# GateLoop attention and a feed-forward block: fp32 weights through the load queue, rotated tiles in one operation, a new order table

## The chip, the cores and the metric

The kernel runs on one core of a Trainium2 chip. The metric is the device time of one execution in microseconds (us), the median of several runs. A core has a matrix engine (PE; its weight loads are shown apart as PEld), a vector engine (DVE), a scalar engine (ACT), a general engine (POOL) and a queue engine (SP) that does nothing here but issue DMA transfers. Sixteen DMA engines carry all transfers.

## What is computed

The inputs q, k, v, a_re, a_im are 4 batches x 8 heads x 768 steps x 48 in fp32. The recurrence keeps a complex 48 x 48 state for each batch and head, decays its rows by the gate a (magnitude capped at 0.999), adds k times v and reads it with q. The heads side by side give x (384 wide), which goes through a normalization, two matrix products with a rectifier between them, and a residual sum:

```
S_re, S_im = ar*S_re - ai*S_im + outer(k_t, v_t), ar*S_im + ai*S_re
y_t = q_t @ S_re                                   # x: the heads' y_t side by side
xn  = (x - mean) / sqrt(var + 1e-6) * g_ln
out = x + max(xn @ w_ch1, 0) @ w_ch2               # 384 -> 1536 -> 384
```

The two weights are fp32 in memory, 2.36 MB each. The kernel computes with them in bf16.

## The kernel before

**Work and names.** A batch of 768 steps is six chunks of 128 steps. Two chunks are a pair `P`, so there are 12 pairs and 24 chunks `n`; `X` is a pair and its part, and only pair 0 has two parts (`PARTS`), split over heads. For each pair the gate gives decays and angles: `ln`, `iv`, `r`, `r2`, `u`, `l`, `lc` work out log magnitude and tangent, `dec` sums the logs on PE, `e` and `en` are its exponentials, `th` and `ph` the angles and their sums, `car` hands the angle to the next pair, `sin`, `abs`, `cos` (or `qt`, `cos` in pairs 0 to 3) fill `trig`.

**Rotated tiles.** `ke` and `qe` are k and q times their decay. `ks` and `qs` (L291 through the helper `tt`) hold, for each head, 48 columns times cosine, 16 zero columns, 48 times sine, 16 zeros. Each is written by two operations of 128x768 elements, `.0` with cosine and `.1` with sine.

**Chunk work.** `kT`, `qT` turn `ks`, `qs` on PE into PSUM (L592) and `ksT`, `qsT` copy them out. Where the table gives `ksT` or `qsT` to SP, the PE step and the copy are left out and a transposing DMA does it (L597). `am` (L615) is the score matrix, `atm` masks it, `gm` (L643) and `G` carry the state, `y` (L665, L668) is the output, `x` its copy, `xtr` and `xT` turn it, `bn` and `rstd` are the normalization, `mm1` (L719), `relu`, `mm2` (L740), `ot`, `st` the rest.

**Loads.** `k`, `q`, `vf` (192 KB each, L403) and `are`, `aim` (384 KB, L444) are issued by SP. They move in rows of 192 and 384 bytes. The weights come in six parts `wl.0` to `wl.5`: three column blocks of `w1b`, three row blocks of `w2b`. POOL issues them as DMAs (L363, L365), and these turn fp32 into bf16 on the way. `wp` and `wc` then fold the mean and `g_ln` into `w1b`, so `wl.0` to `wl.2` must be there before the first `mm1`, and `wl.3` to `wl.5` before `mm2`.

**Order.** Nothing is scheduled at run time. The string `PLAN` lists 1,087 steps with the engine of each (`P`, `A`, `V`, `G`, `S` for PE, ACT, DVE, POOL, SP) and its PSUM bank; each engine runs its own steps in the order of the string and waits at a step until its inputs are there. `@name` holds a POOL step back until the named step of DVE is done. `warm` steps are PE products whose result is not used. `RINGS` gives the number of buffers of each tile; a step that writes a buffer waits for the last user of its previous content. SP is one such engine: a load behind a transposing DMA whose `ks` isn't ready waits with it.

Of the kernel before, what the change touches and what calls it, by code (L numbers as in the profile page):

```python
# [57 lines left out]
en.2.0:A4 ks.0.1.0:G wc.0.1:V3 qT.0:P0 iv.3.0:A wc.0.0:V3 v.0:G kT.0:P1 e.2.0:A4 wc.0.2:V3 warm.71:P2
pad.qs.1:G qsT.0:A0 qT.1:P4 ksT.0:V1 r.3.0:G vf.1.1:S kT.1:P5 qsT.1:V4 car.1.0:A6 am.0:P2 ksT.1:V5 vf.1.0:S
ph.2.0:P0 atm.0:V2 qe.1.0.1:G am.1:P4 q.2.1:S tab.trig.3:A sin.1.0:A6 ke.1.0.0:G atm.1:V4 gm.0:P2 sin.2.0:A0  # L60
are.4.0:S qt.1.0:P6 ke.1.0.1:G y.0:P3 cos.1.0:A6 qt.2.0:P0 G.0:V2 wp.2:P4 ks.1.0.1:V x.0:A3 q.2.0:S cos.2.0:A0
y.1:P5 ks.1.0.0:V xtr.0:P3 qs.1.0.1:V gm.1:P2 aim.4.0:S x.1:A5 kT.3:P6 qs.1.0.0:V th.3.0:A kT.2:P5 G.1:V2
v.1:G@qs.1.0.0 xtr.1:P7 xT.0:A3 qT.2:P0 ksT.2:V5 k.2.0:S xT.1:A7 qT.3:P1 wl.3:G ksT.3:V6 mm1.0.0.1:P2 qsT.3:V1
mm1.0.0.0:P2 r2.3.0:G qsT.2:V0 tab.log.4:A ln.4.0:A am.3:P6 wc.2.1:V4 mm1.0.1.1:P0 relu.0.0:A2 wl.4:G atm.3:V6
mm1.0.1.0:P0 u.3.0:A gm.2:P5 qe.2.0.1:G wc.2.2:V4 am.2:P2 relu.0.1:A0 ph.3.0:P6 wl.5:G wc.2.0:V4 iv.4.0:A
G.2:V5 mm1.0.2.1:P0 qe.2.0.0:G atm.2:V2 y.3:P4 r.4.0:G mm1.0.2.0:P0 car.3.0:V6 y.2:P2 x.3:V4 tab.trig.5:A
sin.3.0:A6 mm2.0.0:P3 x.2:V2 relu.0.2:A0 xtr.3:P4 qs.2.0.0:G bn.1:V qt.3.0:P6 gm.3:P5 mm2.1.0:P2 xT.3:V4
cos.3.0:A6 k.2.1:S xtr.2:P4 mm2.0.1:P3 r2.4.0:A pad.ks.2:G xT.2:V4 q.3.0:S G.3:V5 qs.2.0.1:G mm2.1.1:P2
th.4.0:A bn.3:V mm1.1.0.1:P0 vf.2.0:S bn.2:V mm1.1.2.1:P6 bn.0:V are.6.0:S rstd.1:G mm1.1.2.0:P6 tab.log.6:A
u.4.0:A l.3.0:V mm2.0.2:P3 rstd.0:G k.3.1:S relu.1.2:A6 mm1.1.0.0:P0 l.4.0:V mm1.1.1.1:P4 relu.1.0:A0 q.3.1:S  # L70
lc.3.0:V ke.2.0.1:V mm1.1.1.0:P4 ke.2.0.0:V are.5.0:S dec.3.0:P6 relu.1.1:A4 ks.2.0.1:V mm2.2.0:P0 lc.4.0:V
ks.2.0.0:V ln.6.0:A mm2.2.1:P0 k.3.0:S ot.0:V3 e.3.0:A6 mm2.2.2:P0 vf.2.1:S en.3.0:A6 qT.4:P1 qe.3.0.0:V
kT.4:P3 qe.3.0.1:V iv.6.0:A st.0:S dec.4.0:P4 qs.3.0.1:V aim.5.0:S qsT.4:A1 mm2.1.2:P2 qs.3.0.0:V ksT.4:V3
dps.3:P6 ke.3.0.1:G@qs.3.0.0 en.4.0:A4 qT.5:P7 vf.3.1:S ot.2:V0 mm2.3.0:P1 ln.5.0:A ke.3.0.0:G qsT.5:V7
q.4.0:S qT.6:P0 e.4.0:A4 decc.3:V6 ks.3.0.1:V kT.5:P3 oa.1:A2 am.4:P6 qsT.6:V0 vf.3.0:S v.2:G@ks.3.0.1
ph.4.0:P4 iv.5.0:A ksT.5:V3 ks.3.0.0:G k.4.0:S atm.4:V6 gm.4:P0 car.4.0:A4 am.5:P2 G.4:A0 aim.6.0:S mm2.3.1:P1
atm.5:V2 r.5.0:G kT.6:P0 qT.7:P6 q.4.1:S y.5:P7 tab.trig.7:A sin.4.0:A4 qsT.7:V6 kT.7:P2 ot.1:G k.4.1:S x.5:A7
y.4:P3 ksT.7:V2 th.5.0:A mm2.3.2:P1 v.3:G x.4:V3 vf.4.0:S abs.4.0:A4 dps.4:P6 ksT.6:V0 qe.4.0.0:G xtr.4:P7
am.7:P2 r2.5.0:A xT.4:V7 q.5.0:S xtr.5:P0 decc.4:V6 am.6:P4 r.6.0:G ot.3:V1 xT.5:A0 ph.5.0:P6 cos.4.0:A
vf.4.1:S atm.6:V4 mm1.2.1.1:P0 sin.5.0:A6 are.7.0:S ke.4.0.0:G atm.7:V2 y.6:P4 mm1.2.1.0:P0 abs.5.0:A6  # L80
ke.4.0.1:G gm.6:P5 x.6:A4 are.8.0:S mm1.2.2.0:P2 G.6:V5 cos.5.0:A qe.4.0.1:G xtr.6:P4 relu.2.1:V0 y.7:P6
gm.7:P5 q.5.1:S ks.4.0.1:G x.7:A6 mm1.2.2.1:P2 bn.4:V r2.6.0:A xtr.7:P0 mm1.2.0.1:P6 vf.5.0:S xT.7:V0
relu.2.2:A2 xT.6:V4 mm1.2.0.0:P6 qs.4.0.0:G G.7:V5 st.1:S th.6.0:A bn.7:V mm1.3.0.0:P0 k.5.0:S relu.2.0:V6
mm1.3.1.0:P2 ks.4.0.0:G aim.7.0:S mm1.3.2.1:P4 bn.5:V mm1.3.2.0:P4 tab.log.8:A u.5.0:A bn.6:V rstd.2:G
mm1.3.1.1:P2 u.6.0:A qs.4.0.1:V mm2.5.0:P6 l.5.0:V relu.3.2:A4 qsT.9:S mm2.4.0:P7 mm1.3.0.1:P0 lc.5.0:V
relu.3.1:A2 l.6.0:V ksT.8:S mm2.4.1:P7 ln.7.0:A relu.3.0:V0 dec.5.0:P4 vf.5.1:S mm2.4.2:P7 e.5.0:A4 q.6.1:S
lc.6.0:V v.4:V mm2.5.1:P6 en.5.0:A4 st.3:S qe.5.0.1:V dec.6.0:P2 ot.4:V7 k.5.1:S iv.7.0:A mm2.6.0:P0 en.6.0:A2
r.7.0:G k.6.1:S qT.8:P1 kT.9:P7 ln.8.0:A qsT.8:V1 mm2.5.2:P6 aim.8.0:S e.6.0:A2 ksT.9:V7 am.8:P4 qe.5.0.0:G
r2.7.0:A mm2.7.0:P1 atm.8:V4 st.4:S gm.8:P7 rstd.3:A qs.5.0.0:G st.2:S am.9:P2 u.7.0:A G.8:V7 aim.9.0:S
mm2.6.1:P0 atm.9:V2 ph.6.0:P4 ke.5.0.0:G k.6.0:S qs.5.0.1:V y.9:P2 tab.trig.9:A th.7.0:A gm.9:P7 l.7.0:V  # L90
y.8:P3 q.6.0:S mm2.7.1:P1 abs.6.0:A4 x.9:V2 ke.5.0.1:G@l.7.0 mm2.6.2:P0 are.9.0:S car.6.0:A4 G.9:V7 sin.6.0:A4
mm2.7.2:P1 x.8:V3 qe.6.0.1:V oa.6:A0 qT.11:P7 vf.6.0:S bn.8:V xtr.8:P2 xtr.9:P3 ph.7.0:P4 lc.7.0:V xT.9:A3
q.7.1:S xT.8:V2 cos.6.0:A ks.5.0.0:V mm1.4.1.1:P2 abs.7.0:V4 vf.6.1:S ke.6.0.1:G@ks.5.0.0 car.7.0:A4
mm1.4.1.0:P2 sin.7.0:A4 ks.5.0.1:V dps.6:P0 qsT.10:S oa.7:A1 v.5:V mm1.4.0.1:P4 relu.4.1:A2 ke.6.0.0:V
mm1.4.0.0:P4 qsT.11:V7 ot.6:G@ke.6.0.0 k.7.1:S kT.11:P1 relu.4.0:V4 mm1.4.2.0:P2 ks.6.0.0:G k.7.0:S
mm1.4.2.1:P2 decc.6:V0 tab.log.10:A ln.9.0:A ksT.11:V1 mm2.8.0:P7 q.7.0:S relu.4.2:A2 ot.5:V6 qe.6.0.0:G
kT.10:P0 bn.9:V am.11:P4 k.8.1:S iv.8.0:A qs.6.0.0:G mm2.9.0:P6 ksT.10:V0 rstd.4:A st.6:S dec.7.0:P2 atm.11:V4
iv.9.0:A st.5:S mm2.8.1:P7 k.8.0:S e.7.0:A2 r.8.0:V gm.10:P0 mm2.9.1:P6 en.7.0:A2 ks.6.0.1:V am.10:P4 G.10:A0
qs.6.0.1:V ksT.13:S mm2.8.2:P7 r.9.0:V qT.13:P0 mm2.9.2:P6 atm.10:V4 qsT.12:S ke.7.0.0:G@r.9.0 tab.trig.11:A
th.9.0:A y.11:P1 kT.12:P2 ke.7.0.1:G th.8.0:A x.11:V1 q.8.0:S y.10:P3 qsT.13:V0 ksT.12:A2 xtr.11:P1 ks.7.0.1:G  # L100
ph.8.0:P4 x.10:V3 cos.7.0:A xT.11:V1 xtr.10:P0 ph.9.0:P2 abs.8.0:V4 xT.10:A0 ks.7.0.0:G ot.8:V7 mm1.5.0.1:P0
# [704 lines left out]
```

## Time and profile before

| | |
|---|---|
| time, median of 3 runs | 192.32 us (192.16 to 192.44) |
| span of the profiled execution, first to last instruction | 190.8 us |
| what lies around the span, median less span | 1.5 us |
| busy: PE, DVE, ACT, POOL | 174.8, 154.8, 157.3, 109.9 us |
| DMA queue of SP, packets' time as a share of 16 engines' span | 86.2% |
| DMA queue of POOL, the same | 8.3% |

A time of its own for the profiled execution isn't listed beside its span; the 1.5 us are taken as fixed. The DMA shares add up the times of single packets, so two packets under way in one engine count twice, and a stretch can show a share over 1.

### The profile page before, as it was taken

To read this page: it belongs to the slowest core of one execution; us is meant where nothing else is said; L and a number is where in the kernel's file an instruction comes from. 1 tells how busy PE (TensorE), PEld (TensorE's weight loads), DVE (VectorE), ACT (ScalarE), POOL (GpSimd) and SP (SyncE) were. 2 spreads that over 40 slices of the span, in tenths; PEclk is the share of its full clock that TensorE was granted. 3 is DMA by queue.
4 is the path that set the end of the run, shared out by engine and by line. 5 is a ranking of instruction groups with operands and counts; after the bars stand their busy time and mean duration, and the time that the engine had idled before them with its cause. 6 is when DMAs were issued, how large, how long until landed. Compare 5 with 4: busy or idle time off the path is not lost.

```text
span 190.8 us, 5173 instructions
## 1 busy us (share of the span) xinstructions
PE 174.8 (92%) x2061; PEld 134.5 (70%) x2061; DVE 154.8 (81%) x283; ACT 157.3 (82%) x217; POOL 109.9 (58%) x128
## 2 busy tenths in 40 slices
...
GB/s 140 290 226 220 204 207 192 204 193 200 203 240 201 228 236 219 115 221 255 246 147 240 150 241 272 188 190 144 227 205 145 185 186 172 239 121 164 45 124 84
DMA packets 129768, 36.78 MB, mean 193 GB/s; under 512 B 123984, under 2 KB 129744, under 8 KB 129744
## 3 DMA queue, kind: packets, MB, share of 16 engines
q1 hardware_dynamic: 126960, 34.09, 86.2%
q0 software_dynamic: 2784, 2.36, 8.3%
q8 instruction: 16, 0.26, 0.6%
...
## 4 chain that ended last, share of the span: by engine, by line
PE 50%; DMA 15%; DVE 9%; ACT 6%; POOL 6%; SPq 6%; issue 4%; POOLq 0%; DVEq 0%; ACTq 0%
PE banks L740 17%; PE banks L719 14%; DMA aim<-in_a_im_dram 5%; DMA w2b<-in_moe_w_ch_dram 4%; PE banks L592 4%; SPq L403 3%; PE banks L615 3%; PE banks L495 3%; DMA are<-in_a_re_dram 2%; PE banks L476 2%; DMA qsT<-qs 2%; DVE atm L291 2%; DMA q<-in_q_dram 2%; POOL r L291 2%; PE banks L665 2%
## 5 line engine op out<-in xcount | busy, mean ns | idle before, releaser
L740 PE MATMUL banks<-w2b,h 128*128 128x384 bf16 x288 | 55.3, 326 | 0.3 <-DMA w2b<-in_moe_w_ch_dram 0.3
L719 PE MATMUL banks<-xT,w1b 128*128 128x256 bf16 x432 | 51.3, 273 | 0.9 <-ACT trig L513 0.9
L719 PEld LDWEIGHTS <-w1b 128*128 128x128 bf16 x432 | 41.4, 98 | 7.3 <-issue 0.8
L740 PEld LDWEIGHTS <-h 128*128 128x128 bf16 x288 | 25.8, 97 | 13.5 <-issue 0.4
L291 DVE TENSOR_TENSOR atm<-banks,mask 128x1024 bf16<-128x1024 f32 x24 | 28.8, 1218 | 3.6 <-PE banks L615 3.5
L730 ACT ACTIVATE h<-banks 128x1024 bf16<-128x1024 f32 x26 | 26.0, 1019 | 5.7 <-PE banks L719 4.4
L291 POOL TENSOR_TENSOR ke<-k,en 128x384 bf16<-128x384 f32 x19 | 17.2, 916 | 16.8 <-DVE qs L291 5.8
L774 ACT ACT_TABLE_LOAD x19 | 24.4, 1283 | 1.1 <-PEq L790 0.8
L291 POOL TENSOR_TENSOR ks<-ke,trig 128x768 bf16<-128x768 bf16 (+1 forms) x12 | 18.9, 1583 | 6.6 <-DVE qs L291 2.0
L752 POOL TENSOR_TENSOR ot<-ot,x 128x384 f32<-128x384 f32 x7 | 6.4, 916 | 18.2 <-ACT ot L745 15.9
L291 POOL TENSOR_TENSOR qs<-qe,trig 128x768 bf16<-128x768 bf16 (+1 forms) x10 | 15.7, 1569 | 0.3
L754 DVE SCALAR_TENSOR_TENSOR ot<-banks,rstd,x 128x384 f32<-128x384 f32 x17 | 10.3, 610 | 6.8 <-ACT h L730 3.5
L615 PE MATMUL banks<-qsT,ksT 128*128 128x128 bf16 x192 | 14.6, 219 | 1.1 <-DVE ksT L288 0.9
L291 POOL TENSOR_TENSOR qe<-q,e 128x384 bf16<-128x384 f32 x14 | 12.7, 918 | 4.2 <-ACT trig L513 3.4
L615 PEld LDWEIGHTS <-ksT 128*128 128x128 bf16 x192 | 12.0, 98 | 3.2 <-DVE ksT L288 1.0
L291 POOL TENSOR_TENSOR r<-aim,are 128x768 f16<-128x768 f32 x6 | 10.9, 1816 | 5.5 <-ACT are L449 5.4
L476 PE MATMUL banks<-l,u_e 128*128 128x384 f16 (+1 forms) x52 | 10.9, 342 | 3.5 <-DVE l L468 3.4
L732 DVE TENSOR_SCALAR h<-banks 128x1024 bf16<-128x1024 f32 x10 | 12.1, 1216 | 2.0 <-PE banks L719 2.0
L678 DVE BATCH_NORM_STATS2 stats<-x 128x6 f32<-128x384 bf16 x24 | 13.1, 547 | 0.0
L769 PE MATMUL banks<-u_e 128*128 128x256 f16 x72 | 11.1, 312 | 2.2 <-POOL u_e L325 2.2
L447 ACT ACTIVATE w<-are 128x768 f32<-128x768 f32 (+1 forms) x13 | 10.1, 794 | 3.4 <-DMA are<-in_a_re_dram 3.3
L665 PE MATMUL banks<-v,atm 128*128 128x48 bf16 x192 | 12.1, 183 | 0.1
...
## 6 DMA issues: line engine op xcount, KB each, us to landing
...
```

What stands on the lines that cost most here:

```text
L291: {"DVE": nc.vector, "POOL": nc.gpsimd}[eng(name)].tensor_tensor(**kw)
L476: nc.tensor.matmul(heads(ps[:, c]), lhsT=u_e[:, c, j], rhs=step(T("l", P), j), start=(j == 0), stop=(j == R - 1))
L615: nc.tensor.matmul(ps[:, h], lhsT=T("ksT", n)[:, h], rhs=T("qsT", n)[:, h], start=True, stop=True)
L665: nc.tensor.matmul(ps[:, h], lhsT=T("atm", n)[:, h], rhs=T("v", P)[:, c, h], start=True, stop=nfirst)
L678: nc.vector.bn_stats(out=T("stats", n), in_=T("x", n))
L719: nc.tensor.matmul(ps[:, jj], lhsT=w1b[:, dc, ts(gi * JG + jj, C)], rhs=T("xT", P)[:, dc].rearrange("p c t -> p (c t)"), start=(dc == 0), ...
L730: act(out=dst, in_=src, func=AF.Relu)
L732: nc.vector.tensor_scalar(out=dst, in0=src, scalar1=0.0, scalar2=None, op0=ALU.max)
L740: nc.tensor.matmul(bank(f"o.{n}")[:, 0:DM], lhsT=T("h", P)[:, j, ts(c, C)], rhs=w2b[:, j], start=(j == 0), stop=(j == NJ - 1))
L754: nc.vector.scalar_tensor_tensor(out=T("ot", n), in0=bank(f"o.{n}")[:, 0:DM], scalar=T("rstd", P)[:, ds(c, 1)], in1=T("x", n), op0=ALU.mul ...
L769: g.add(f"warm.{i}", lambda i=i: nc.tensor.matmul(bank(f"warm.{i}")[:, 0:256], lhsT=u_e[:, 0, 0], rhs=u_e[:, 1].rearrange("p j t -> p (j t ...
L774: g.add(f"tab.{nm}.{i}", lambda tab=tab: nc.scalar.preload_act_table_set(tab))
```

## The change

1. **Weights.** Six new DMAs `wf.0` to `wf.5` on SP bring the fp32 weights into two staging buffers. `wl.0` to `wl.5` become casts: `wl.0` on DVE, `wl.1` on ACT, the other four on POOL.
2. **Rotated tiles.** A step `ks.P.i.2` or `qs.P.i.2` does the cosine and the sine part in one DVE operation on 1,536 elements. The table uses it for 9 of the `ks` and 8 of the `qs`.
3. **`lc`** may run on POOL; the table puts 8 of 13 there.
4. **A new table** of 1,141 steps. SP gets 30 transposing DMAs (15 `ksT`, 15 `qsT`) where it had 22 (12 and 10), PE has 18 `kT` and `qT` where it had 26, and 142 `warm` where it had 72. `ks` and `qs` on POOL fall from 22 to 4. Two chunks (16 and 19) mask on POOL after a copy `ac` on ACT.

The diff without the old table, and with the new one cut:

```diff
-         "mv": 5, "rstd": 5, "xT": 3, "h": 2, "ot": 3, "car": 2}
+         "mv": 5, "rstd": 5, "xT": 3, "h": 2, "ot": 3, "car": 2, "wf": 2}
+WEIGHTS = (0, 1, 2, 3, 4, 5)
 PLAN = """
+are.0.1:S tab.log.0:A ln.0.1:A iv.0.1:A aim.0.1:S r.0.1:V are.0.0:S ln.0.0:A iv.0.0:A aim.0.0:S ue:G pad.ks.0:G
+r2.0.1:V one:G pad.qs.1:G u.0.1:A wf.0:S r.0.0:V r2.0.0:A l.0.1:V lc.0.1:V wl.0:V warm.0:P0 warm.1:P0 warm.2:P0
...
+dec.0.1:P0 u.0.0:A are.1.0:S cmean:G uth:V gln:S aim.1.0:S are.2.0:S en.0.1:A0 pad.qs.0:G ln.1.0:A iv.1.0:A
...
+aim.4.0:S qsT.0:V2 vf.1.0:S iv.4.0:A decc.1:V0 ksT.0:V3 ksT.1:V6 qt.1.0:P4 tab.trig.3:A cos.1.0:A4 decc.0:V1
+qsT.1:V7 warm.132:P0 warm.133:P0 am.0:P2 atm.0:V2 wp.2:P0 r.3.0:G ph.2.0:P6 th.3.0:A wc.2.1:V0 am.1:P2 r.4.0:V
+vf.0.0:S q.2.1:S sin.2.0:A6 v.0:V vf.1.1:S wc.2.2:V0 k.2.1:S th.4.0:A warm.134:P1 warm.135:P1 warm.136:P1
...
+k.2.0:S gm.0:P1 y.0:P0 G.0:A1 gm.1:P1 x.0:A0 ks.1.0.2:V wf.3:S v.1:G@ks.1.0.2 cos.2.0:A6 qt.3.0:P4 r2.3.0:G
+atm.1:V2 r2.4.0:G are.5.0:S cos.3.0:A4 kT.2:P0 qT.3:P6 qT.2:P7 ksT.2:V0 dec.2.0:P4 xtr.0:P0 G.1:V1 kT.3:P1
+qsT.2:V7 tab.log.4:A u.3.0:A gm.2:P2 xT.0:A0 e.2.0:A4 qsT.3:V6 ksT.3:V1 l.3.0:V lc.3.0:G@l.3.0 en.2.0:A4
+warm.141:P3 am.2:P6 wl.3:G atm.2:V6 y.1:P3 x.1:A3 ph.4.0:P0 am.3:P4 G.2:A2 xtr.1:P3 wf.4:S wl.4:G gm.3:P2
+atm.3:V4 xT.1:A3 dec.3.0:P6 G.3:V2 y.2:P3 mm1.0.0.1:P4 ke.2.0.1:G y.3:P2 ln.5.0:A q.2.0:S x.2:V3 abs.4.0:V0
...
 """
-            assert name.split(".")[0] in ("kT", "qT", "xtr", "oa", "ac", "tab", "warm"), name
+            assert name.split(".")[0] in ("kT", "qT", "xtr", "oa", "ac", "tab", "warm", "ks", "qs"), name
+              "wf": ([C, 1536], FP32)}
-    for i in range(NG):
-        g.add(f"wl.{i}", lambda i=i: nc.gpsimd.dma_start(
-            out=w1b[:, :, ts(i, 512)], in_=moe_w_ch1.rearrange("(dc p) j -> p dc j", p=C)[:, :, ts(i, 512)]))
-        g.add(f"wl.{NG + i}", lambda i=i: nc.gpsimd.dma_start(
-            out=w2b[:, ts(i, JG)], in_=moe_w_ch2.rearrange("(jc p) e -> p jc e", p=C)[:, ts(i, JG)]))
+    halves = [(w1b[:, :, ts(i, 512)], moe_w_ch1.rearrange("(dc p) j -> p dc j", p=C)[:, :, ts(i, 512)], ND)
+              for i in range(NG)] + [(w2b[:, ts(i, JG)], moe_w_ch2.rearrange(
+                  "(jc p) e -> p jc e", p=C)[:, ts(i, JG)], JG) for i in range(NG)]
+    turn = {i: k for k, i in enumerate(WEIGHTS)}
+    for i, (dst, src, n) in enumerate(halves):
+        def stage(i=i, n=n):
+            return T("wf", turn[i]).rearrange("p (a x) -> p a x", a=n)
+        g.add(f"wf.{i}", lambda src=src, stage=stage: nc.sync.dma_start(out=stage(), in_=src),
+              uses=[("wf", turn[i])])
+
+        def f_wl(i=i, dst=dst, stage=stage):
+            if eng(f"wl.{i}") == "ACT":
+                nc.scalar.copy(out=dst, in_=stage())
+            else:
+                {"DVE": nc.vector, "POOL": nc.gpsimd}[eng(f"wl.{i}")].tensor_scalar(
+                    out=dst, in0=stage(), scalar1=1.0, scalar2=0.0, op0=ALU.mult, op1=ALU.add)
+        g.add(f"wl.{i}", f_wl, needs=[f"wf.{i}"], uses=[("wf", turn[i])])
-            add(f"lc.{X}", lambda S_=S_: nc.vector.tensor_scalar(
+            add(f"lc.{X}", lambda S_=S_, X=X: {
+                "DVE": nc.vector, "POOL": nc.gpsimd}[eng(f"lc.{X}")].tensor_scalar(
+                def f_both(nm=nm, src=src, X=X):
+                    tt(f"{nm}.{X}.2", out=T(nm, P).rearrange("p c h (a x) -> p (c h) a x", a=2)[:, :, :, 0:D],
+                       in0=T(src, P).rearrange("p c (h d) -> p (c h) d", d=D).unsqueeze(
+                           2).to_broadcast([C, R * H, 2, D]),
+                       in1=T("trig", P).rearrange("p a c (h d) -> p (c h) a d", d=D), op=ALU.mult)
+                if NS == 1:
+                    add(f"{nm}.{X}.2", f_both, needs=[f"{src}.{X}.{m}" for m in range(2)]
+                        + [f"cos.{X}", f"sin.{X}"], uses=[(src, P), ("trig", P), (nm, P)])
-            return [f"{nm}.{P}.{i}.{a}" for i in range(NS) for a in range(2)]
+            return [f"{nm}.{P}.{i}.{a}" for i in range(NS) for a in range(3)]
-    for i in range(72):
+    for i in range(142):
```

The steps of SP in the new table stand in this order up to the last weight part, and then at the end: `are.0.1 aim.0.1 are.0.0 aim.0.0 wf.0 are.1 gln aim.1 are.2 wf.1 aim.2 k.0.0 q.0.0 q.1.1 q.0.1 k.0.1 k.1.1 k.1.0 q.1.0 wf.2 are.3 are.4 aim.3 vf.0.1 aim.4 vf.1.0 vf.0.0 q.2.1 vf.1.1 k.2.1 k.2.0 wf.3 are.5 wf.4 q.2.0 vf.2.1 aim.6 aim.5 are.6 q.3.1 vf.2.0 wf.5` and `st.13 qsT.20 k.11.1 ksT.20 ksT.21 qsT.21 q.11.0 st.15 st.14 vf.11.1 vf.11.0 ksT.23 qsT.23 qsT.22 ksT.22`, followed by stores alone.

More of the change, by code (lines that the diff above doesn't have):

```diff
@@ L58 @@
[L58 to L101, printed above, removed]
-sin.9.0:A2 ot.9:V6 st.8:S mm1.5.0.0:P0 car.9.0:A2 q.8.1:S abs.9.0:V2 ot.7:G sin.8.0:A4 mm1.5.1.0:P6 are.10.0:S
@@ new lines @@
+mm2.2.1:P1 ksT.4:V6 qsT.5:S q.4.1:S am.5:P2 en.4.0:A4 mm2.2.2:P1 k.4.0:S ph.5.0:P6 qsT.4:S am.4:P4 k.4.1:S
+bn.0:V atm.5:V2 y.5:P2 tab.trig.7:A cos.4.0:A r.6.0:G th.6.0:A atm.4:V4 qe.4.0.1:G mm2.1.0:P3 mm2.0.2:P0
+mm2.1.1:P3 qs.3.0.2:V x.5:A2 xtr.5:P2 abs.5.0:A6 rstd.1:G rstd.0:G q.5.0:S qT.7:P4 ke.4.0.0:V mm2.1.2:P3
+aim.7.0:S ks.3.0.2:V oa.2:A1 y.4:P1 bn.5:V mm2.3.0:P5 sin.5.0:A6 are.8.0:S r2.6.0:A vf.3.0:S xT.5:V2 are.7.0:S
+qsT.7:V4 ph.6.0:P6 qT.6:P4 ot.1:V3 ot.2:G@ks.3.0.2 r2.5.0:G cos.5.0:A mm2.3.1:P5 x.4:A1 q.4.0:S qe.4.0.0:G
@@ new lines @@
+xtr.4:P1 sin.6.0:A6 ot.0:V0 aim.8.0:S qsT.6:V4 dps.3:P0 mm2.3.2:P5 xT.4:V1 mm1.2.0.1:P2 decc.3:V0 dps.4:P4
+q.5.1:S tab.log.8:A u.6.0:A mm1.2.1.1:P0 abs.6.0:V6 ke.4.0.1:G u.5.0:A vf.3.1:S bn.4:V mm1.2.0.0:P2 v.3:G
+mm1.2.1.0:P0 car.6.0:A6 decc.4:V4 ks.4.0.2:V qs.4.0.2:V mm1.2.2.0:P6 relu.2.0:A2 relu.2.1:A0 mm1.2.2.1:P6
+relu.2.2:A6 ksT.6:S st.0:S am.6:P2 rstd.2:G l.5.0:V atm.6:V2 lc.5.0:G@l.5.0 mm2.5.0:P4 ksT.7:S ln.7.0:A iv.7.0:A
+oa.3:A5 k.5.1:S l.6.0:V k.5.0:S mm2.4.0:P0 gm.6:P1 r.7.0:G@l.6.0 mm2.5.1:P4 am.7:P2 ln.8.0:A ot.3:G G.6:V1
@@ new lines @@
+lc.6.0:G dec.5.0:P6 e.5.0:A6 vf.4.0:S y.6:P5 en.5.0:A6 atm.7:V2 mm2.5.2:P4 y.7:P2 vf.4.1:S qe.5.0.1:G qe.5.0.0:G
+x.6:V5 bn.6:V gm.7:P1 x.7:V2 kT.9:P5 ksT.9:V5 xtr.6:P6 st.2:S ke.5.0.1:G qT.8:P7 qsT.8:V7 r2.7.0:A u.7.0:A
+ot.5:V4 iv.8.0:A xT.6:V6 ke.5.0.0:G mm2.4.1:P0 dec.6.0:P2 en.6.0:A2 ksT.8:S vf.5.1:S xtr.7:P7 qsT.9:S e.6.0:A2
+mm2.4.2:P0 am.8:P4 xT.7:V7 mm1.3.0.0:P6 q.6.1:S G.7:V1 tab.trig.9:A cos.6.0:A am.9:P2 mm1.3.0.1:P6 atm.8:V4
+q.6.0:S aim.9.0:S are.10.0:S relu.3.0:A6 k.6.0:S v.4:G are.9.0:S mm1.3.2.0:P4 atm.9:V2 aim.10.0:S gm.8:P1
```

141 lines of the change are left out of this document (82 added, 59 removed).

## The prediction

> **What bounds the kernel now.** I read the page first, then the windows, then the chain that ended last and the groups by shape.
>
> ```profile
> span 190.8 us, 5173 instructions
> ...
> PE 174.8 (92%) x2061; PEld 134.5 (70%) x2061; DVE 154.8 (81%) x283; ACT 157.3 (82%) x217; POOL 109.9 (58%) x128
> ...
> q1 hardware_dynamic: 126960, 34.09, 86.2%
> q0 software_dynamic: 2784, 2.36, 8.3%
> ```
>
> PE is at 92%, but the two DMA queues together hold 94.5% of the engines' time: two resources, not one, are nearly full. The windows place this:
>
> ```profile
> core 0: us, PE busy (x) PEld busy (x) DVE busy (x) ACT busy (x) POOL busy (x), PEclk, DMA share, GB/s
> 46.00:186.50 140.50, 138.57 (x1652) 106.72 (x1650) 119.68 (x215) 117.49 (x161) 81.22 (x77) 1.00 0.94 191
> 186.50:190.80 4.30, 0.00 (x0) 0.00 (x0) 0.65 (x2) 0.00 (x0) 0.00 (x0) 0.84 0.26 93
> 54.00:76.00 22.00, 22.00 (x322) 18.12 (x320) 20.19 (x37) 21.05 (x30) 17.95 (x16) 1.00 0.99 223
> 78.00:126.00 48.00, 47.09 (x565) 36.37 (x563) 43.30 (x74) 45.04 (x63) 30.33 (x27) 1.00 1.06 216
> 126.00:174.00 48.00, 47.30 (x574) 36.16 (x572) 40.32 (x73) 36.99 (x51) 25.93 (x25) 1.00 1.02 185
> ```
>
> From 46 to 186.5 us PE idles 1.9 us of 140.5; then 4.3 us follow in which the last rows leave. Before 46 it waits for loads and for DVE and ACT. The DMA share is 1 all the while. The chain shows DMA on the end's path:
>
> ```profile
> 163.07 3.74 DMA q<-in_q_dram
> ...
> 168.18 0.55 DVE qs L291
> ...
> 168.76 4.06 DMA qsT<-qs
> ...
> 172.86 0.61 PE banks L615 x8
> ...
> 183.24 3.26 PE banks L740 x20
> ...
> 186.53 0.62 DVE ot L754
> ```
>
> The last q is loaded, multiplied, transposed by DMA, and only then do the last scores (`am`, L615) start, at 172.86; 17.9 us later all is over. So the end is the later of two sums: PE's work after its start, and the DMA work up to the last transposing DMA plus some 17 us.
>
> **Prices of DMA work.** From the packets of the trace (size, time; 16 engines): a load of q, k or v is 1,024 packets of 192 B at 15.7 ns, 1.00 us. One of `are` or `aim` is 1,024 of 384 B at 24.0 ns, 1.54; the stretch 2 to 18 us moved 6.0 of the one and 7.0 of the other, which gives 1.39; I take 1.45. A store is 128 packets of 1,536 B at 69.5 ns, 0.55. A transposing DMA isn't seen alone. The last two windows, 96 us, hold 38 loads, 7 of `are`/`aim`, 15.7 stores and 22 transposing DMAs; 96 - 38 - 10.2 - 8.6 = 39.2 us, 1.78 each if DMA never idles. The densest stretch, 170 to 174, did 2.5 of them and 1.7 stores, 1.25 each. I take 1.5, as the windows contain idle DMA.
>
> **Weights.** POOL's casting DMAs go: 0.083 x 190.8 = 15.8 us of DMA. Each `wf` moves 768 KB in rows of 1.5 or 2 KB. The nearest row is the store, 1,536 B in 69.5 ns: 512 x 69.5 / 16 = 2.2 us. Bounds: 1.4 (it can't beat a load of half its size) and 2.6 (the casting DMA). Six are 13.2, so DMA gains 2.6 us (-0.2 to 7.4). But they stand in SP's order: `vf.0.0`, 17th on SP now, gets 2,304 KB of weights ahead of it. The casts: 1,536 elements, by the `v` rows of 768 (DVE 0.55, ACT 0.83, POOL 0.83) about 1.0, 1.5 and 1.6 us. They wait for their `wf`; behind `wl.0` on DVE stand `uth` and `l.0.0`, behind `wl.1` on ACT `en.1.0`, behind `wl.2` on POOL `qe.1.0.0`. `wf.0` arrives near 8 us, when DVE gets there; this costs under 1 us, before loads that come later anyway. On SP `wf.2` to `wf.5` wait for casts that are done earlier than the queue gets to them.
>
> **Rotated tiles.** Rows:
>
> ```profile
> L291 POOL TENSOR_TENSOR ks<-ke,trig 128x768 bf16<-128x768 bf16 x11 | 18.0, 1643 | 6.6 <-DVE qs L291 2.0 <-issue 1.7 <-PE banks L668 1.4
> ...
> L291 DVE TENSOR_TENSOR ks<-ke,trig 128x768 bf16<-128x768 bf16 x11 | 6.1, 566 | 0.8 <-POOL ke L291 0.8
> ```
>
> With 384 elements DVE takes 0.354, so 0.55 ns an element, and 1,536 take 0.99 (bounds: 0.85 with no fixed part, 2.0 at the fp32 slope of the `r` rows, 0.554 for 384 and 1.039 for 768). DVE before: 24 x 0.566 + 6 x 0.354 = 15.7. After: 17 x 0.99 + 6 x 0.566 + 8 x 0.354 = 23.0, 7.3 more. It loses 8 `lc` (0.37), 4 copies of `ksT`/`qsT` (0.68), 2 `atm` (1.22), 3 `v` (0.55) and small ones, 8.5. Net -1; POOL -9 (34.6 us of `ks`, `qs` become 6.6; casts, `lc`, `r2`, masks come), ACT -5. None is the later one after 46 us, where DVE idles 20.8 us and ACT 23. These edits I cost at nothing; PE's full stretch hides them.
>
> **Transposing DMAs.** PE loses 8 `kT`/`qT` of 0.45 (L592 x8 in the chain): 3.6 us on the path while PE is last. DMA gets 8 x 1.5 = 12 us (10 to 14.2).
>
> **Sum for PE.** Adding the chain's pipelined prices over each table (six `mm1` products 0.66, four `mm2` 0.65, `am`, `kT`, `qT` 0.45, `dec` 0.65, `ph` 1.0, `y` 0.43, `gm` 0.2, `xtr` 0.17) gives 160.4 us before, 156.8 after, `warm` apart. In the new table 19.4 of it stands ahead of `mm1.0.0.1`; when does that start? DMA prices put the end of `k.1.0` at 22.4, so DVE gets to `ke.1.0.0` at 23. Up to `v.0` it has 12.6 us: 13 pieces of 0.35 to 0.57 (8 `ks`/`qs`, 5 `ke`/`qe`), `car`, 4 copies of 0.68, `decc`, `atm.0`, one `wc`, `r.4`. That is 35.6; `vf.0.0` lands near 35. From `v.0` to `atm.2` DVE has 10.7 more (2 `wc`, 2 doubled tiles, 2 `atm`, 4 copies, `G`, `l`). ACT, by the same adding, gets to `xT.1` at 46.7. So `mm1.0.0.1` starts at 47 (45 to 50); before it was 36.6, though with less attention work done. Then 137.4 us of PE, and 2.9 as the old table took over its own sum from 46.4 on: 187.3, plus 4.3: span 191.6.
>
> **Sum for DMA.** Up to the last transposing DMA the new order has 72 x 1.00 + 24 x 1.45 + 30 x 1.5 + 6 x 2.2 + 16 x 0.55 + 0.3 = 174.1; begun at 2.0, it ends at 176.1 without any idle time. The old table by the same prices: 166.7 where 172.8 was seen, 6 us idle; late DMA waits less, so 1.5: 177.5. From there PE has `am.22` and 11.6 us of its order, 0.7 of waits and the 4.3: span 194.6. DMA is the later one. With the 1.5 us around the span that stands between 190.8 and the median 192.32, I forecast 196.1.
>
> A rule speaks against this price: the Trainium skill, page "Advanced Engine Details and Errata", section X-Bar Transpose (TRN2), says that transposing DMAs are as fast as ordinary ones, 350 to 400 GB/s. A tile is 262 KB, so that estimate is 0.7 us each, 24 us less DMA in all, and PE alone would decide. The trace differs: 1.25 us at its densest.
>
> **Rivals.**
> - DMA keeps up and PE decides with `mm1` at 47: 191.6 + 1.5 = 193.1, slower still. It needs 1.3 us or less per transposing DMA. For: the dense stretch, and DMA that ran ahead of PE before. Against: the old table's 6 idle us are the only reserve, and 12 are asked.
> - Faster: DMA keeps up, and PE's saved 3.6 us show. The place is the start of `mm1.0.0.1`: every us there is one at the end. It decides below 45.8 (45.8 + 137.4 + 2.9 + 4.3 + 1.5 = 191.9); at 45 with 2 us of waits it gives 190.2. For: the order has all four first chunks done by then and puts 142 `warm` into the gaps. Against: DVE's sum has no wait in it and gives 46.7.
> - The doubled operation runs at the fp32 slope: 17 x 1.0 = 17 us more DVE. Half hides in its 20.8 idle us: 193.1 + 8 = 201. For: it is a pattern with a repeated operand that no row has. Against: inner runs of 48 bf16 as in the 566 ns row.
>
> **How the numbers follow.** Forecast 0.50 (194 to 202: 1.4 to 1.7 us per transposing DMA); first rival 0.17; faster rival 0.22, and 0.05 for its upper edge, within 0.2% (0.4 us, about what a measurement tells from none); slow operation 0.06. So faster 0.22, same 0.05, slower 0.73. The range is 190.2, the faster rival's price, to 202.
>
> **What would show it.** Right: `am.22` not before 176; SP's queue over 92% of a longer span, POOL's queue gone; PE idle over 5 us between 100 and 180, ended by `ksT` or `qsT` of DMA; `mm1` first at 46 to 48; doubled tiles near 1.0 us. Wrong: PE idle under 3 us after 50 with transposing DMAs landing before 172, or `mm1` first before 45.

## The result, and the profile after

The changed kernel takes 210.72 us (median of 4, 210.21 to 213.03) beside 192.38 for the kernel before: a ratio of 1.099 [1.093, 1.106], slower. The forecast was 196.1, in a range up to 202.0. Times here are medians of all executions and ratios compare undisturbed ones only; where e7, e9 and e18 were profiled the execution was a disturbed one, so their rows serve for order and not for small differences.

From the page of the changed kernel: span, busy time by engine, TensorE's granted clock in 40 slices, the queue.

```profile
span 208.3 us, 5173 instructions
...
PE 183.7 (88%) x2065; PEld 139.4 (67%) x2067; DVE 159.7 (77%) x270; ACT 155.7 (75%) x211; POOL 116.4 (56%) x125
...
PEclk9979999999999999999969999999999969999999
...
q1 hardware_dynamic: 138192, 40.91, 92.6%
```

SP's queue is at 92.6% and POOL's is gone, as forecast. The clock row has two slices at 6, near 104 and 166 us; the kernel before has none below 9 between 20 us and its end. The first `mm1` (now L749) starts at 49.5 us, where it started at 36.6. Windows from there on:

```profile
core 0: us, PE busy (x) PEld busy (x) DVE busy (x) ACT busy (x) POOL busy (x), PEclk, DMA share, GB/s
49.50:204.30 154.80, 142.86 (x1650) 108.48 (x1646) 119.97 (x200) 116.04 (x153) 97.70 (x88) 0.98 0.94 186
...
60.00:100.00 40.00, 36.02 (x464) 27.62 (x463) 33.22 (x59) 35.09 (x44) 31.99 (x30) 1.00 1.09 219
100.00:112.00 12.00, 7.93 (x50) 5.07 (x48) 6.67 (x12) 7.23 (x10) 8.35 (x8) 0.86 0.86 185
112.00:160.00 48.00, 46.63 (x589) 35.59 (x588) 42.47 (x72) 40.44 (x54) 35.89 (x30) 1.00 1.04 195
160.00:180.00 20.00, 17.74 (x183) 13.69 (x182) 12.86 (x23) 11.91 (x18) 9.83 (x9) 0.91 0.83 134
```

PE idles 154.80 - 142.86 = 11.9 us behind its start (1.9 in 149.9 before). In its longest idle stretch the others idle too: between 100 and 112 us every engine is below 70%, DMA at 0.86. Nothing is full there; the steps wait for each other. (From 60 to 100 us, where PE idles 4.0, the DMA share is 1.09.) The list of waits names the longest:

```profile
PE banks L497 <- POOL l L489: 5.8, 4, 2.3
...
DVE ot L784 <- DMA out_dram<-ot: 5.0, 1, 5.0
...
PE banks L497 <- DVE ot L784: 4.1, 1, 4.1
```

L497 is `dec`, L489 is `lc`, L784 is `ot`. The chain of the stretch 95 to 112 shows how the longest of these comes about:

```profile
100.64 1.43 SPq L423
...
102.11 2.90 DMA out_dram<-ot
...
105.03 0.63 DVE ot L784
...
105.71 1.46 PE banks L497 x4
```

SP comes to an old chunk's store only at 102.1, behind loads (L423). It lands at 105.0. Only then may DVE write the next `ot` into that buffer (there are three), `dec.7.0` needs the PSUM bank that this `ot` empties, and PE stands still for 4.07 us. No DMA row looks late by itself: it is the place of a store in SP's order, behind a backlog of loads. SP issues without a pause from 88 to 102 us, and one load takes it 0.6 to 1.9 us there, where the first four loads of the kernel took 0.45 to 0.51.

The groups by shape:

```profile
L489 POOL TENSOR_SCALAR l<-l 128x768 f16<-128x768 f16 x8 | 22.4, 2804 | 4.9 <-DVE ks L299 2.3 <-DVE l L485 2.2
...
L299 DVE TENSOR_TENSOR ks<-ke,trig 128x1536 bf16<-128x1536 bf16 x9 | 9.2, 1017 | 0.6 <-POOL ke L299 0.6
L299 DVE TENSOR_TENSOR qs<-qe,trig 128x1536 bf16<-128x1536 bf16 x8 | 7.6, 952 | 0.3 <-POOL qe L299 0.2
...
L489 DVE TENSOR_SCALAR l<-l 128x768 f16<-128x768 f16 x3 | 1.1, 355 | 0.0
```

The doubled tile costs what was forecast (0.95 to 1.02 us). `lc` on POOL takes 2.80 us where DVE takes 0.355.

The busy times of the first page line are off the forecast too: DVE went up by 4.9 us (154.8 to 159.7) where -1 was expected, ACT down by 1.6 and not 5, POOL up by 6.5 and not down by 9.

### The profile page after: what moved, and what is told of

The parts are those of the page before. It is cut to its first block, busy times and chain, and to the rows that moved or that the text cites. A ratio compares the mean times of both kernels' runs of the same rounds, so it can differ in the third digit from the quotient of the medians.

```text
span 208.3 us, 5173 instructions
## 1 busy us (share of the span) xinstructions
PE 183.7 (88%) x2065; PEld 139.4 (67%) x2067; DVE 159.7 (77%) x270; ACT 155.7 (75%) x211; POOL 116.4 (56%) x125
## 3 DMA queue, kind: packets, MB, share of 16 engines
q1 hardware_dynamic: 138192, 40.91, 92.6%
## 4 chain that ended last, share of the span: by engine, by line
PE 39%; SPq 18%; DMA 15%; DVE 12%; POOL 9%; issue 4%; DVEq 0%; ACT 0%; POOLq 0%; ACTq 0%
PE banks L770 14%; PE banks L749 13%; SPq L464 10%; SPq L423 6%; DMA qsT<-qs 5%; DMA vf<-in_v_dram 4%; DMA aim<-in_a_im_dram 3%; POOL l L489 3%; PE banks L645 3%; DMA ksT<-ks 3%; POOL r L299 2%; PE banks L497 2%; DVE l L485 2%; DVE w1b L407 2%; PE banks L516 2%
## 5 line engine op out<-in xcount | busy, mean ns | idle before, releaser
L749 PE MATMUL banks<-xT,w1b 128*128 128x256 bf16 x432 | 53.8, 277 | 1.2 <-ACT xT L294 0.9
L749 PEld LDWEIGHTS <-w1b 128*128 128x128 bf16 x432 | 41.7, 99 | 8.6 <-issue 1.9
L299 DVE TENSOR_TENSOR atm<-banks,mask 128x1024 bf16<-128x1024 f32 x22 | 26.8, 1220 | 10.2 <-PE banks L645 9.9
L489 POOL TENSOR_SCALAR l<-l 128x768 f16<-128x768 f16 x8 | 22.4, 2804 | 4.9 <-DVE ks L299 2.3
L299 POOL TENSOR_TENSOR qe<-q,e 128x384 bf16<-128x384 f32 x16 | 14.6, 913 | 16.4 <-DMA q<-in_q_dram 9.7
L497 PE MATMUL banks<-l,u_e 128*128 128x384 f16 (+1 forms) x52 | 11.4, 349 | 12.1 <-POOL l L489 5.8
L799 PE MATMUL banks<-u_e 128*128 128x256 f16 x142 | 19.6, 299 | 2.2 <-POOL u_e L333 2.2
L799 PEld LDWEIGHTS <-u_e 128*128 128x128 f16 x142 | 15.1, 107 | 5.9 <-POOL u_e L333 1.8
L784 DVE SCALAR_TENSOR_TENSOR ot<-banks,rstd,x 128x384 f32<-128x384 f32 x16 | 9.5, 610 | 11.0 <-DMA out_dram<-ot 5.0
L501 ACT ACTIVATE en<-banks 128x768 bf16<-128x768 f32 (+1 forms) x13 | 9.9, 758 | 9.6 <-PE banks L497 9.6
L433 POOL TENSOR_SCALAR v<-vf 128x768 bf16<-128x768 f32 x10 | 8.7, 865 | 14.5 <-DVE ks L299 11.9
L299 POOL TENSOR_TENSOR r<-aim,are 128x768 f16<-128x768 f32 x7 | 12.7, 1811 | 5.3 <-ACT th L505 2.9
L497 PEld LDWEIGHTS <-u_e 128*128 128x128 f16 x52 | 5.1, 104 | 15.5 <-issue 9.1
L299 POOL TENSOR_TENSOR ke<-k,en 128x384 bf16<-128x384 f32 x16 | 14.5, 914 | 1.7 <-ACT en L501 1.0
L299 DVE TENSOR_TENSOR ks<-ke,trig 128x1536 bf16<-128x1536 bf16 (+2 forms) x17 | 13.7, 819 | 0.9 <-POOL ke L299 0.6
```

Source lines behind the costliest of these rows:

```text
L299: {"DVE": nc.vector, "POOL": nc.gpsimd}[eng(name)].tensor_tensor(**kw)
L489: "DVE": nc.vector, "POOL": nc.gpsimd}[eng(f"lc.{X}")].tensor_scalar(
L497: nc.tensor.matmul(heads(ps[:, c]), lhsT=u_e[:, c, j], rhs=step(T("l", P), j), start=(j == 0), stop=(j == R - 1))
L749: nc.tensor.matmul(ps[:, jj], lhsT=w1b[:, dc, ts(gi * JG + jj, C)], rhs=T("xT", P)[:, dc].rearrange("p c t -> p (c t)"), start=(dc == 0), ...
L799: g.add(f"warm.{i}", lambda i=i: nc.tensor.matmul(bank(f"warm.{i}")[:, 0:256], lhsT=u_e[:, 0, 0], rhs=u_e[:, 1].rearrange("p j t -> p (j t ...
```

## The experiments

Ratios are to the kernel before in the same runs. "First" is the start of the first `mm1`.

| run | us | ratio | first, us |
|---|---|---|---|
| changed kernel | 210.72 | 1.099 [1.093, 1.106] | 49.5 |
| e1 | 208.41 | 1.082 [1.074, 1.089] | 49.6 |
| e2 | 204.91 | 1.064 [1.059, 1.068] | 36.3 |
| e3 (one execution) | 208.73 | - | 47.7 |
| e4 | 206.57 | 1.074 [1.069, 1.078] | 48.6 |
| e5 | 210.01 | 1.092 [1.083, 1.100] | 49.6 |
| e6 | 205.87 | 1.070 [1.062, 1.078] | 50.5 |
| e7 | 227.66 | 1.180 [1.169, 1.190] | 48.3 |
| e8 | 206.35 | 1.070 [1.061, 1.079] | 36.3 |
| e9 | 214.67 | 1.112 [1.103, 1.121] | 49.5 |
| e10 | 204.77 | 1.065 [1.058, 1.072] | 50.5 |
| e11 | 196.24 | 1.022 [1.016, 1.029] | 39.3 |
| e12 | 203.95 | 1.062 [1.056, 1.068] | 49.1 |
| e13 | 192.25 | 0.999 [0.995, 1.003] | 36.2 |
| e14 | 204.16 | 1.064 [1.059, 1.069] | 46.5 |
| e15 | 202.13 | 1.055 [1.048, 1.062] | 50.3 |
| e16 | 202.41 | 1.052 [1.044, 1.060] | 50.7 |
| e17 | 209.14 | 1.091 [1.084, 1.097] | 47.5 |
| e18 | 202.00 | 1.049 [1.041, 1.058] | 49.8 |

**The caps: e1, e2, e3.** e1 puts the eight `lc` of the changed table back on DVE; e2 puts the same eight on POOL in the old table, with nothing else; e3 replaces the minimum of the changed kernel's POOL `lc` by a product, so it leaves the cap out there. (In e2 three POOL steps also lose their `@lc`.)

```diff
 e1, table:  -lc.3.0:G@l.3.0           +lc.3.0:V          (8 such steps)
 e2, table:  -lc.3.0:V                 +lc.3.0:G          (8 such steps, old table)
 e3, POOL:   -scalar1=LNCAP, op0=ALU.min    +scalar1=1.0, op0=ALU.mult
```

> The changed kernel with all eight lc steps that the new table gives to POOL put back on DVE, at the same places of the table; nothing else. Theory A (an lc on POOL takes 2.80 us where I had booked 0.83, and it stands between l and dec, so each of the eight holds up the decay of its pair and the queue of POOL): the time falls to 195 to 198 us, the DMA-bound forecast. Theory B (the SP queue alone: transposing DMAs, loads and stores waiting for each other in one order): still 205 or more, PE idle under L497 gone but PE idle under DMA as before. Theory C (the start of the first mm1 at 49.5 us): 208 or more.

> The kernel before with one part of the change alone: the lc of pairs 3 and 5 to 11 on POOL, at the same places of the old table. Theory A: 22 us more on POOL and 2.4 us more in each of eight decay chains; 196 to 204 us. Theory B: the old table has slack in POOL (81 of 140 us busy after 46 us), so under 193.5 us.

> The changed kernel, lc on POOL as in its table, but there with a product by 1.0 where the minimum stood: the cap of the magnitude is left out in those eight pairs. If the minimum is what is dear on POOL, one lc falls from 2.80 us to 0.8 to 0.9 like v (768 elements, product and sum, 0.87), and the time is that of the kernel with lc on DVE within 2 us, 195 to 199. If the fp16 type or writing in place is what is dear, it stays 2.8 us and the time stays at 210.

In e3 one `lc` on POOL takes 0.83 us at the median, so the minimum is what is dear. The row, beside 2,804 ns above:

```profile
L489 POOL TENSOR_SCALAR l<-l 128x768 f16<-128x768 f16 x8 | 6.8, 855 | 4.9 <-DVE ks L299 2.3 <-DVE l L485 2.2
```

Alone in the old table the dear `lc` costs 12.7 us (204.9 in all, just above theory A's 204). The waits of e2 show it (L472 is `dec`, L464 `lc`):

```profile
PE banks L472 <- POOL l L464: 7.1, 4, 2.5
```

Taken out of the changed table it gives back only 2.3, so theory A of e1 is out. PE's gaps under `lc` are gone in e1, and others are longer or new. The timeline of e1, idle time before each piece in brackets:

```profile
81.64 0.62 PE L641 MATMUL banks<-qsT,ksT 128*128 128x128 bf16 x8 [2.28 <-DMA ksT<-ks]
88.08 0.20 PE L691 MATMUL banks<-v,atm 128*128 128x48 bf16 x1 [1.73 <-DVE atm L295]
```

The gap under `ksT` was 1.35 in the changed kernel, the one under `atm` was not there, and the one under `ot` went from 4.07 to 4.35. `lc` on DVE isn't always cheap in this order either: in e1 the seven that ran beside no POOL operation took 0.26 to 0.36 us, and the six that ran beside one took 0.45 to 1.78. Two lines of the timeline show one of them (before, 12 of the 13 stayed at 0.36 or below):

```profile
44.83 2.27 POOL L380 TENSOR_SCALAR w2b<-wf 128x1536 bf16<-128x1536 f32 x1
...
45.81 1.51 DVE L485 TENSOR_SCALAR l<-l 128x768 f16<-128x768 f16 x1
```

So e1 compares a dear `lc` with one that is partly dear, and 2.3 us is not the whole price of the minimum in the new order.

**The doubled tiles: e4, e13.** e4 is e1 with each of the 17 doubled steps split in two DVE steps at its place. e13 puts the doubled form alone into the old table, for seven tiles.

```diff
 e4, table:   -ks.5.0.2:V     +ks.5.0.0:V ks.5.0.1:V      (17 such)
 e13, table:  -ks.5.0.0:V ... -ks.5.0.1:V     +ks.5.0.2:V  (7 such, old table)
```

> The changed kernel with lc on DVE and the 17 doubled tiles split again into a cosine and a sine operation, both on DVE at the same place. The doubled operation took 1.02 and 0.95 us, two single ones 2 x 0.566 = 1.13. If the doubled form is worth only its saved fixed part (17 x 0.13 = 2.3 us of DVE, mostly beside other work), the time is that of the kernel with lc on DVE, 0 to 1 us more. If it sits on the path, 2 to 3 us more. If the doubled form hurts (one long operation holding DVE or POOL), 1 us or more less.

> The kernel before with the doubled form alone: seven tiles (ks of pairs 1, 2, 5; qs of pairs 1, 3, 8, 11) whose two halves VectorE makes one after the other there become one operation each, at the place of the second half. If one operation costs what two cost (0.99 against 2 x 0.5 to 0.6 us): 191.5 to 193. If the later readiness of the first half counts in the old order as the other parts do: 194 or more.

e4 is 1.8 us below e1, and the intervals of the two touch, so only this much is sure: the doubled form gains nothing here. e13 can't be told from the kernel before. The form is not where the time went.

**The transposing DMAs: e5, e8.** e5 is e1 with the eight tiles back on PE, the copies in turn on DVE and ACT, next to where the transposing DMAs stood and in the first bank that is free. e8 moves the same eight from PE to SP in the old table.

```diff
 e5, table:  -ksT.6:S              +kT.6:P6 ksT.6:V6     (8 tiles)
 e8, table:  -kT.6:P0 ... ksT.6:V0    +ksT.6:S           (8 tiles, old table)
```

> The changed kernel with lc on DVE, and eight of the 30 transposing DMAs (qsT 4, 5, 15, 16 and ksT 6, 7, 10, 12) taken back to PE and a copy on DVE or ACT, so that SP has 22 as before. Theory B (DMA and the SP queue run late; the lag of the queue against the sum of its transfers was 12 us at the last transposing DMA, and PE, stores and output buffers wait for it): 194 to 199 us, 9 to 14 less than with lc on DVE alone; the wait of ot for its store's DMA is gone. Theory C (the start of mm1 at 49.5 us and the new order itself): 206 or more, as PE gets 3.6 us more.

> The kernel before with one part of the change alone: the same eight tiles (qsT 4, 5, 15, 16 and ksT 6, 7, 10, 12) go to transposing DMAs of SP, 30 in all, at the places where PE's transposes stood. PE has 3.6 us less. Theory B: DMA gets 12 us more, where the old table had some 6 us idle, and each wait comes back through SP's order: 198 to 206 us. If DMA has room, 189 to 192.

In the old table the eight cost 14.4 us, and it is the landing of a few of them that PE waits for (waits of e8, L610 is `am`):

```profile
PE banks L610 <- DMA qsT<-qs: 6.9, 1, 6.9
...
PE banks L610 <- DMA ksT<-ks: 5.5, 2, 4.3
```

These are two long gaps, 6.9 and 4.3 us, so the 14.4 us are not the transfer time of eight transposes. In the changed table their removal gives nothing: e5 has 1.6 us more than e1, with intervals that overlap. The waits on `ksT` became waits for the copies on ACT. So my theory that DMA volume ends the changed kernel failed here. One reserve: I placed the steps by hand, and a better place may gain.

**The weights: e6, e11, e14.** e6 is e1 with POOL's casting DMAs at the table's places of `wf`. e11 is the old kernel with fp32 loads on SP and six casts on POOL. e14 is the changed kernel without the six loads, with constants written in place of the casts.

```diff
 e6, table:   -wf.2:S ... -wl.2:G@qe.1.0.1    +wl.2:G     (6 such; wl is the casting DMA again)
 e11, table:  -wl.2:G@qs.0.0.0    +wf.2:S ... +wl.2:G     (6 such, old table)
 e14, code:   -lambda src=src, stage=stage: nc.sync.dma_start(out=stage(), in_=src)    +lambda: None
```

> The changed kernel with lc on DVE, and the weights by casting DMAs issued from POOL as before, at the places of the table where SP's fp32 loads stood; no staging buffers, no casts. If the weights in SP's queue delay the head (6.6 us of transfers ahead of the v of pair 0), the first mm1 moves from 49.5 to 44 to 46 us and the time falls by 3 to 5 us. If the DMA engines are the limit, whoever issues, it stays within 2 us of the kernel with lc on DVE.

> The kernel before with the change's weights alone: fp32 through SP's queue into two staging buffers, six casts on GpSimd, loads near the places where the casting DMAs stood, the last two behind the casts that free their buffers. Theory A (each part costs when put alone into the old order): 194 to 198, about 10 us of casts on GpSimd and the loads ahead of others in SP's queue. Theory B (the weights are cheap, what costs is the order): 191 to 194.

> The changed kernel without the six weight loads (14 us of transfer, half of it before the first pair's v is loaded); constants are written in place of the casts. If the transfers set the late start of the expert layer: its first product at 45 us or earlier (49.5 in the changed kernel) and 202 to 206 in all. If VectorE's and ScalarE's fixed order ahead of it set the start: first product after 48 and 207 or more.

e11 prices the part alone at 4.4 us; its first `mm1` is 2.7 us later. In the changed table the casting DMAs are 2.5 us better than e1 by the medians, with intervals that overlap, though the start is no earlier (50.5), and with no weight loads at all (e14, 6.6 us less than the changed kernel) the start comes at 46.5. That is 3 of the 12.9 us of delay; e14's total was the one theory's and its start neither's.

**Stores and output buffers: e7, e12.** e7 is e1 with the 24 stores issued by POOL. e12 is e6 with six `ot` buffers.

```diff
 e7, code:   -nc.sync.dma_start(out=out[b]...      +nc.gpsimd.dma_start(out=out[b]...
 e12, code:  -"ot": 3                              +"ot": 6
```

> The changed kernel with lc on DVE, and the 24 stores of the output issued by POOL instead of SP, at the same places of the table. The DMA work is the same; the order of SP no longer holds stores behind loads, nor loads and transposing DMAs behind a store that waits for its row. If SP's one order is what costs (SP waited, output buffers were not free): 4 to 10 us less than with lc on DVE alone. If the sum of DMA work is what costs: within 2 us of it.

> The changed kernel with caps on VectorE and the weights by casting DMAs (e6, 205.9 us), and six output buffers ot instead of three (the staging buffers' room is used). e6 shows 4.5 us in which VectorE waits to write ot until an old chunk's store has landed, and TensorE 3.5 us behind it. If that wait is real loss: 202 to 203.5. If it only stands where another wait would be (transfers, steps in order): 204.5 to 206.5.

e7 lost 19 us, which no theory had: POOL, too, runs in order and now waits for the rows (POOL waits 20.6 us for `ot`). e12 is 1.9 us below e6, with touching intervals; the 4.5 us wait of `ot` is gone from its rows. By the medians the stall was worth about half its length.

**Fewer transfers, and the named causes off: e9, e10, e15, e16.** e9 takes all four parts back at once and leaves the new order, its 142 `warm` steps among it. e10 leaves out 24 loads. e15 and e16 join the edits of e1, e4, e6 and e12, e15 with those 24 loads left out as well. Where loads are left out, old data are used.

```diff
 e10, e15:  add(f"{nm}.{P}.{c}", lambda ...: None if P >= 4 and c == 1 else nc.sync.dma_start(...
```

> The changed kernel with all four other parts undone at once: the caps on VectorE, the seventeen doubled tiles split in two, the eight tiles back on TensorE (copies in turn on VectorE and ScalarE), the weights by GpSimd's casting DMAs. Only the new order of the steps is left. Theory A (the parts carry the loss, and single undoings gave only 2 us each because another part took over): 191 to 196. Theory B (the order itself carries most of it: the first product of the expert layer starts at 49.5 us where the kernel before has it at 36.6, and 141 us of TensorE's work plus 7 us of tail and edges come behind it, so 199 at the least): 199 to 206, with the first such product after 47 us.

> The changed kernel without 24 of its 72 loads of q, k and vf (second chunk of pairs 4 to 11; old data are used in their place): about 24 us of transfer less behind 50 us, nothing else changed. If the lag of the transfers behind their sum (12 us at the last transposing DMA) is what ends the kernel: 193 to 199, and the waits on ksT and qsT go. If TensorE's late start and the steps in order on the other engines set it: 203 or more, although the DMA share falls by a tenth.

> The changed order with every named cause off at once: caps on VectorE, casting DMAs, six output buffers, the doubled tiles split in two, and 24 loads less (old data in their place). If these are the loss behind the expert layer's first product: 194 to 198 (first product at 49, then 137.4 of TensorE's units, 2.9 of edges, 4.3 of tail, 1.5 around the span), with no wait of TensorE over 2 us behind 50 us. If the order makes new waits whenever one is taken away: 201 or more.

> As the run before, with all loads kept (caps on VectorE, casting DMAs, six output buffers, doubled tiles split). If transfers still set the end: 3 to 6 us above that run. If TensorE's late start and other engines set it: within 2 us of it. By the sum of what single steps gave (2.3, 2.5, 1.9 and 1.8 us off 210.7): 202.

e10 gains 6 us, and its gap under `ot` is gone: with less ahead of it in SP's queue the store goes out in time. Where the causes have been removed otherwise, the same 24 us of transfers are worth nothing. Stretch 60 to 180 us of e15, then of e16:

```profile
60.00:180.00 120.00, 114.24 (x1394) 87.92 (x1393) 106.79 (x196) 101.02 (x133) 69.34 (x72) 1.00 0.86 165
```

```profile
60.00:180.00 120.00, 114.11 (x1387) 87.63 (x1385) 107.30 (x196) 100.88 (x132) 69.75 (x73) 1.00 1.08 204
```

DMA share 0.86 against 1.08, and PE's busy time is the same to 0.13 us. Transfers are thus not the bound of this order; they matter where a step on SP stands behind them and somebody needs that step. e16 also checks the sum: 2.3, 2.5, 1.9 and 1.8 off 210.7 make 202.2, and it takes 202.4. Three of the four terms lie within the overlap of two intervals; the sum of 8.3 is clear of noise.

The undoing has a price of its own. In e6, e12, e15, e16 and e18 a `mm2` (L756 in e16) waits 2.7 to 3.1 us for a part of `w2b` that the casting DMAs bring late; in the changed kernel this wait is not there. From e16:

```profile
67.44 0.81 PE L756 MATMUL banks<-w2b,h 128*128 128x384 bf16 x4 [2.91 <-DMA w2b<-in_moe_w_ch_dram]
```

e9 differs from e16 by PE's transposes and by three output buffers in place of six, and it is no better than the changed kernel itself (the intervals just overlap); both theories of e9 had less. SP there waits 27.9 us for `ot` rows before its stores, in six waits. With this order, taking the parts back does not bring the old time back.

**The start: e17, e18.** Up to the first `mm1` DVE has 25.5 us of work in the kernel before and 38.6 in the changed one, 13.1 more, close to the delay of 12.9. To test it, e17 (changed kernel) and e18 (e16) leave the nine `wc` out.

```diff
-g.add(f"wc.{jb}.{ec}", lambda jb=jb, ec=ec, o=o: nc.vector.scalar_tensor_tensor(...
+g.add(f"wc.{jb}.{ec}", lambda: None, needs=[o], ps=(o, 1))
```

> The changed kernel without the nine operations that scale and centre w1b on VectorE (wc; 6.3 us, all ahead of the expert layer's first product; the weights are used unscaled). Up to that product VectorE has 38.6 us of work in the changed kernel and 25.5 in the one before, 13.1 more, and the product starts 12.9 us later. If VectorE's work ahead of it paces the start: first product at 43.5 to 46 (49.5 now), and 204 to 207 in all. If loads or ScalarE pace it: 48 or later, and 208 or more.

> The same nine operations left out of e16 (every named cause off, all loads; first product at 50.7, 202.4 us). If the start sets what is left there: first product at 45 to 47 and 197 to 199. If the start is earlier and the end is not: the loss behind it, 5 us in e16, grows by as much, and TensorE's rows show new waits.

The start moved by 2.0 us in e17 and by less in e18, not by 5: DVE alone does not pace it. ACT's work ahead of the first `mm1` grew as well, from 30.7 to 39.7 us, and PE's from 26.8 to 40.4; all of PE's 142 `warm` steps stand there (19.6 us busy, before 11.1). In the changed kernel, from 20 us to the first `mm1`:

```profile
20.00:49.50 29.50, 24.88 (x318) 18.77 (x318) 27.16 (x49) 27.35 (x41) 11.63 (x8) 1.00 1.03 254
```

DVE (third number) and ACT (fourth) are equally full, 27.16 and 27.35 of 29.5 us. What holds the start changes hands along the way. In the changed kernel `v` of pair 0 waits for its load until 37.0, and DVE then works without a pause of note to 44.0. At 47.5 `xT.1` is done; PE's order has `dec.3.0` ahead of `mm1`, and that waits for an `lc` on POOL:

```profile
48.47 0.81 PE L497 MATMUL banks<-l,u_e 128*128 128x384 f16 x4 [1.18 <-POOL l L489]
```

e18's chain runs from the landing of an `are` at 17.3 mostly through ACT operations, with 30 `warm` products in it:

```profile
22.13 4.82 PE banks L783 x30
```

The last 1.2 us of them hold back a `ph` whose `th` is there at 25.56. So `warm`, which the table doubles, is a rival too, and no run took `warm` or ACT work away. How the 12.9 us divide stays open: without the weight loads the start is 3.0 us earlier, without `wc` 2.0.

## Why the prediction was wrong

The sign was right (0.73 for slower) and the size not: 14.6 us short. The sign owes something to luck: DMA's sum, which gave the 196.1, is not what made the kernel slow. PE's sum, with the late start in it, came to 193.1, slower by little. By its own steps:

- **Start of `mm1`.** Forecast 47 (45 to 50), measured 49.5. This term gave 2.5 us too little. DVE reached `ke.1.0.0` at 24.7, not 23, and `vf.0.0` landed at 37.0, not near 35. ACT was added up too, to 46.7 for `xT.1`, but as if it never waited; `xT.1` was done at 47.5, and `dec.3.0` behind `lc` came before `mm1`.
- **Work behind the start.** 137.4 + 2.9 + 4.3 = 144.6 forecast; measured 158.8. The 2.9 for waits became 11.9 of idle PE, 9.0 more. Gaps over 0.5 us hold 11.0 of it: 4.07 under `ot` and its store, 4.6 under `lc`, 1.35 under `ksT`, 0.93 under `xT`. The lowered clock adds 3.1 (below). Some 2.1 stay unassigned. The failed step is "these edits I cost at nothing": it set idle engine time against added work (and the items named in DVE's sum, 8 `lc`, 4 copies, 2 `atm` and 3 `v`, already make 9.8 and not 8.5). In this fixed order that idle time was no cover: e2 shows it alone, where POOL had idle time and 8 late `lc` cost 12.7 us, because PE waits for them.
- **`lc` on POOL.** It stood in one clause ("casts, `lc`, `r2`, masks come") at nothing, priced like `v` at 0.83. It took 2.80. Alone that costs 12.7 us in the old order (e2); put back on DVE in the new one it gives 2.3 (e1).
- **DMA sum.** Forecast: the later of the two, its idle time down to 1.5 us, end at 177.5 for the last transposing DMA and 194.6 in all. The last was issued at 187.3, the last `am` ran at 192.69, so "not before 176" held. But SP waited, 16.1 us for `ot` rows before stores and, at one transposing DMA, 6.7 us for a DVE step (`xT` by the profile), where the sum allowed 1.5 us of idle DMA in all. e16 against e15 shows for their order that volume was not the bound. The step "DMA is the later one" failed. Its price of 1.5 us for a transposing DMA was low as well: by their packets the 30 took 1.80 each, and the 22 before had already taken 1.83, which the trace did show (22,528 packets of 256 B at 28.5 ns). That the 12 us for eight of them (bounds 10 to 14.2) are near the 14.4 of e8 is chance: e8's loss is two gaps of PE.
- **Weights, casts, doubled tiles.** Near their marks but for the cast on DVE, 1.75 (forecast 1.0): the other casts took 1.47 (ACT, POOL; forecast 1.5 and 1.6), doubled tiles 0.95 to 1.02 (0.99). The slow-operation rival is out. The loads take 2.3 to 2.4 us each by their packets (2.2). (The lower bound of DMA's gain, -0.2, should read 0.2: 15.8 less six times 2.6.)
- **Signs.** The first `mm1`, at 49.5, is later than the 46 to 48 given. PE idles over 5 us in 100 to 180, as said, but `ot` and `lc` end these waits, not `ksT` or `qsT`. That sign alone would have told that the mechanism was another.
- **Rivals.** "DMA keeps up, PE decides" is nearest: DMA's volume does not bind. But its time, 193.1, allowed for 2.9 us of waits and not 11.9. The faster rival needed a start before 45.8.

The Trainium skill, page "Advanced Engine Details and Errata", section X-Bar Transpose (TRN2), has transposing DMAs as fast as ordinary ones. Here the packets of the 30 took 1.80 us of the 16 engines each, beside 1.02 for a load of three quarters of the bytes, a third more by the byte, so the trace does not bear it out for these tiles.

What is left open: e16's span is 9.6 us longer than before (200.4 to 190.8). PE is busy for 148.0 us behind its start in the old order and for 139.4 in e16, 8.6 less: 3.6 of it are transposes gone from PE (by the forecast's units), 5.0 stand ahead of the start instead. So of the 14.1 us by which e16 starts later 9.1 are lost, 3.6 are saved, and idle PE behind the start adds 4.0 (5.9 for 1.9). Of the 5.9, 2.91 are the wait for `w2b`, which e16's own undoing made, and 1.72 one wait for `atm`. No version tried beats the kernel before.
